# A sixth key tile for VectorE in the last 256 queries of a two-layer transformer kernel, with another opening and another order

## The chip, the cores and the metric

The kernel runs on one core of a Trainium2 chip, in one launch. The metric is device time in microseconds (us); lower is better. The engines are TensorE (PE; its weight loads are PEld), VectorE (DVE), ScalarE (ACT), GpSimd (POOL) and SyncE (SP, which issues the DMAs).

## The reference

```python
def reference(A_x, A_wqkv, A_wo, B_x, B_w1, B_b1, B_w2, B_b2):
    # _A_ref: attention, 32 heads of 16, over S=2048 rows of D=512, then @ wo
    #   scores = q k^T / 4;  p = softmax(scores);  o = p v
    # _B_ref: gelu(x @ w1 + b1) @ w2 + b2, hidden width F=1792
    x = A_x
    x = x + _A_ref(_layernorm(x, axis=-1), A_wqkv, A_wo)
    x = x + _B_ref(_layernorm(x, axis=-1), B_w1, B_b1, B_w2, B_b2)
    x = x + _A_ref(_layernorm(x, axis=-1), A_wqkv, A_wo)
    x = x + _B_ref(_layernorm(x, axis=-1), B_w1, B_b1, B_w2, B_b2)
    return x
```

Both layers use the same weights. Inputs and output are bfloat16.

## The kernel before

**Cells.** Attention is cut into cells: 128 keys (one of 16 key tiles `kt`) by 512 columns of scores. A pass is one segment of queries, one group of heads `g`, all 16 key tiles and four row groups `a`, so 64 cells. A segment is 512 queries; the last 512 queries of layer one are two segments of 256, in which a cell holds two heads side by side. There are 2048 cells in each layer. A cell's score is one matmul of 512 columns into a PSUM bank (L1432). Then its exponential is taken in one of two ways:

- ScalarE: one ACTIVATE over two or three banks at once (L1879) writes the unnormalized weights into units of a ring `pt`, or into units lent from other tensors that are dead at the time (`kt`, `q`, `g`, `v` in the profile's names). Then follows one matmul with V (PV).
- VectorE: one tensor_scalar (L1601) turns the scores into the bits of a rough exponential in a buffer `du` (or one lent from `kt`, `v`); GpSimd makes three shifted variants of it with two 64-bit integer adds for each pair of cells (L1691, L1695). Four PV matmuls follow, one with V and three with copies of V scaled by the weights `VW`, which `vcopies` makes (L1363). Only the tiles in `KD[l]` (five in each layer) have such copies and may go this way; a cell of theirs that nobody has taken when a pass runs out goes to ScalarE too.

PV matmuls (L1945) accumulate in one bank; PE puts matmuls with a zero matrix beside them where row groups are missing (L1953), and fillers where it would idle (L1420). In the last two segments PV and the first feed-forward product run in widths of 256 columns.

**Around attention.** When a segment's attention is done, `norm` divides and transposes on VectorE (L1000 to L1018), `wo` projects and adds (L1046), `ln` normalizes (L779 to L828), `hpair` makes the first feed-forward product (14 chunks, 16 matmuls each, L647 through `quads`; VectorE adds b1, L1155, or for the last segment ScalarE does all, L1150), `gelu` runs over half of the chunks at a time (L1176, with a table load before and after), and `ytile` makes the second product and adds (L1207). These run among the next segment's attention; for the last two segments part or all of it is left to the end. The opening loads tiles of x, normalizes the first four with GpSimd's power (L791), transposes them on PE (L844), projects K and Q, and starts.

**What sets the order.** A planner in the kernel, run when the program is built, goes through generators with assumed durations and priorities and writes out one fixed list of instructions and waits for each engine (`_Sched.run`). `KNOBS` are its parameters; `PICKS` chooses a row of `ORDERS` for each `STRETCH` of 24 us of its own clock. `SW` is the assumed cost of a change of PE's tiling mode. [...] On the chip there is no scheduler: each engine runs its list in order and waits for semaphores.

Of the kernel before, what the change touches and what calls it, by code (L numbers as in the profile page):

```python
# [5 lines left out]
ALU = mybir.AluOpType  # L6
ACT = mybir.ActivationFunctionType
BF16 = mybir.dt.bfloat16
# [6 lines left out]
D = 512  # L15
H = 32
# [14 lines left out]
W_MORE = 4  # L31
XT = 8
# [20 lines left out]
NKD = 5  # L53
QAT = (0, 200, 240, 280)
# [56 lines left out]
)  # L111
STRETCH = 24
PICKS = (1, 13, 1, 1, 13, 13, 1, 2, 1, 13, 1, 13, 13, 1, 1, 14, 1, 13, 13, 13, 13, 11, 3, 1,
         1, 13, 13, 13, 13, 13, 13, 1, 13, 13, 13, 1, 13, 1, 1, 1, 1, 3, 13, 13, 5, 1, 13, 13,
         1, 0, 1, 1, 13, 13, 13, 13, 1, 1, 1, 13)
# [141 lines left out]
HOLDP = 0.35  # L257
HOLDT = 0.2
# [5 lines left out]
class _Sched:  # L264
# [5 lines left out]
    def __init__(self, P):  # L270
        self.P = P
        self.clock = {e: 0.0 for e in P.ENGS}
        self.end = {}
# [68 lines left out]
    def _ready(self, op):  # L342
        t = 0.0
        for k in op.reads:
            if k not in self.P.lastw:
                return None
        for ev in self.P.deps(op.reads, op.writes):
            if op.eng == "pe" and ev[0] == "pe":
                continue
            t = max(t, self.end.get(ev, 0.0) - OWN * (op.eng == "dve" == ev[0]))  # L350
        if op.eng == "pe" and op.mode != self.mode:
            t -= SW
        if op.eng == "pool":
            if HOLDP and self.held_off(max(t, self.clock["pool"])):
                op.limit = 0.0
                return None
            if op.limit == 0.0:
                op.limit = self.port_ops[-1][1] + LATENCY["dve"]
            if op.limit < 1e9:
                t = max(t, op.limit)  # L360
            t = max(t, self.last(max(t, self.clock["pool"]))[0])
        if op.port and op.eng == "dve":
            at = max(t, self.clock["dve"])
            for a, b in self.pool_ops[-6:]:
                if a < at + HEAD and at < b - HEAD:
                    at = t = b - HEAD
        return t

# [67 lines left out]
    def run(self):  # L436
        while True:
# [75 lines left out]
SW = 0.107  # L513
# [5 lines left out]
def bass_interleave_layers__mha_block__dense_activation_gelu__prompt_kernel(  # L519
# [15 lines left out]
    with ExitStack() as es:  # L535
# [40 lines left out]
        T["VC"] = sb([128, NKD, 3, H * 17], BF16, "vc")  # L576
# [60 lines left out]
class _Plan:  # L637
# [12 lines left out]
    def init(self):  # L650
# [5 lines left out]
        yield _Op("pool", 0.1, lambda e: e.memset(T["IDENT"][:], 0.0), writes=["IDENT"])  # L656
# [3 lines left out]
        yield _Op("pool", 0.2, lambda e: e.memset(T["DU"][0][:, 0, 0, :].bitcast(BF16), 1.0), writes=["DU.0.0.0"])  # L660
# [6 lines left out]
        yield _Op("dve", 0.1, lambda e: e.tensor_reduce(  # L667
# [388 lines left out]
    def wloads(self):  # L1056
# [16 lines left out]
        for i, (l, seg) in enumerate(order):  # L1073
            todo = [((l, seg, "1", p), cols(hbm["w1"], 256 * p), 2) for p in range(NFC // 2)]
            tail = l == NL - 1 and seg[0] == self.NQ - 1
            if not tail:
                todo += [((l, seg, "2", (t, p)), rows(hbm["w2"], 256 * p, 0, D), 1) for t in self.tiles(seg) for p in range(NFC // 2)]
# [83 lines left out]
    def gelu(self, l, seg):  # L1161
# [8 lines left out]
        for f in range(0, NFC, half):  # L1170
# [4 lines left out]
            yield _Op("act", 0.065 + 0.4267 * half * n / 512 + ((1 if f == 0 else 0) + (0 if f == 0 or tail else 1)) * 1.31,  # L1175
                      lambda e, g=g: e.activation(out=g, in_=g, func=ACT.Gelu_apprx_tanh), reads=gk, writes=gk, prio=2)  # L1176
            for p in range(f // 2, (f + half) // 2):
                yield ("give", ("g", l, seg, p))

    def ytile(self, l, seg, t):  # L1180
# [5 lines left out]
        b = None if tail else (yield ("need", ("w", l, seg, "2", (t, 0))))  # L1186
# [3 lines left out]
        for p in range(NFC // 2):  # L1190
# [4 lines left out]
            else:  # L1195
                piece = (NL - 1, self.segs[NL - 1][-1], "2", last) if tail else (l, seg, "2", (t, p))
# [3 lines left out]
            for j in range(2):  # L1200
                fns += self.quads(pb, T["G"][:, 2 * p + j, q], ws[j], not (p or j), p == last and j == 1)
            yield _Op("pe", len(fns) // 4 * MM, fns, reads=[wk] + ["G.%d.%d" % (f, t % 4) for f in (2 * p, 2 * p + 1)],
                      writes=["B.%d" % b], prio=MID if p else FPRIO, mode="P")
# [119 lines left out]
    def setup_attention(self):  # L1323
# [4 lines left out]
        for pi, (l, seg, g, kts, part, final) in enumerate(self.pas):  # L1328
            self.alist.append([(pi, kt, a) for kt in kts if kt not in KD[l] for a in range(4)])
            self.dlist.append([(pi, kt, a) for kt in kts if kt in KD[l] for a in range(4)])  # L1330
# [5 lines left out]
        self.vuse = {(l, kt): sum(c[1] == kt for p, q in zip(self.pas, self.dlist) if p[0] == l for c in q) for l in range(NL) for kt in KD[l]}  # L1336
# [16 lines left out]

    def vcopies(self):
        T = self.T
        for l in range(NL):
            for j, kt in enumerate(KD[l]):
# [4 lines left out]
                for i, w in enumerate(VW):  # L1362
                    yield _Op("dve", 0.31, lambda e, j=j, i=i, w=w, src=src: e.tensor_scalar(  # L1363
                        T["VC"][:, j, i, :], src, w, 1.0, op0=ALU.mult, op1=ALU.mult),
                        reads=["V%d.%d" % (l, kt), self.vone(l, kt)], writes=["VC.%d.%d" % (j, i)])
                yield ("give", ("vc", l, kt))
            self.lend = 1

# [37 lines left out]
    def filler(self, b, mode):  # L1406
        T = self.T
        src = self.source()
        if src == ["VC.0.0"]:
            lhs, rhs = T["VC"][:, 0, 0, 0:128], T["VC"][:, 0, 0, 0:512]  # L1410
        else:
            lhs, rhs = T["IDENT"], T["DU"][0][:, 0, 0, :].bitcast(BF16)
# [289 lines left out]
    def copied(self, cell, du, jj, i):  # L1702
# [7 lines left out]
        else:  # L1710
            j = KD[l].index(kt)
            ws, wk = [T["VC"][:, j, i - 1, 17 * h:17 * h + 17] for h in hs], ["VC.%d.%d" % (j, i - 1)]
# [81 lines left out]
    def lend_units(self):  # L1794
# [9 lines left out]
        for u in range(*self.blocks[self.gblock - 1]):  # L1804
            yield ("rel", "pt", u)
# [91 lines left out]
    def pvs(self):  # L1897
        T = self.T
        pools = self.s.pools
        for pi, (l, seg, g, kts, part, final) in enumerate(self.pas):  # L1900
# [21 lines left out]
            def build(op, start, pi=pi, b=b, l=l, cols=cols, begun=begun, n=n):  # L1922
                op.fns, op.reads, rounds = [], [], 0
                while rounds < ROUNDS:
# [24 lines left out]
                    if rest and (warm or end):  # L1949
                        rhs = T["VC"][:, 0, 0, 0:512] if warm else T["ONES1"][:, 0:1].to_broadcast([128, 512])  # L1950
# [107 lines left out]
```

## Time and profile before

| What | Value |
|---|---|
| Time, median of 3 runs | 1429.25 us (1429.19 to 1429.66) |
| The profiled execution's own time | 1429.75 us |
| Its span, first to last instruction | 1427.9 us |
| Busy: PE, DVE, ACT, POOL | 1385.5, 1216.6, 1401.1, 997.9 us |
| Granted TensorE clock | 1.00 |
| DMA | 103.47 MB, 72 GB/s on average |

Columns of a row that groups instructions: line, engine, operation, tiles out<-in, shapes, count, then busy time and mean ns of one, then the engine's idle time before them and who ended it. A timeline row has start, duration, engine, line, operation, tiles, count, and in brackets the idle time before it. A row of stages has the stretch, its length, then busy time and instructions of PE, PEld, DVE, ACT and POOL, the clock, the share of DMA and GB/s. A row of waits has who waited, for whom, the total, the number of times and the longest. Records of one engine can overlap, so a duration can be longer than the time that an instruction adds.

### The profile page before, as it was taken

How to read it: one execution, taken by the hardware profiler on the slowest of the kernel's cores; microseconds unless marked ns; L12 is line 12 of the kernel's file. 1: busy time of each engine (PE TensorE's matmuls, PEld its weight loads, DVE VectorE, ACT ScalarE, POOL GpSimd, SP SyncE). 2: the span in 40 equal slices, each digit the busy share in tenths (PEclk: the TensorE clock that was granted, in tenths of full speed). 3: DMA queues.
4: the chain of work that ended last, by engine and by line, in shares of the span. 5: the costliest groups of instructions: out<-in, count | busy, mean ns of one | idle time of the engine just before them, and what ended most of it. 6: DMA issues, size and time to landing. Idle time of an engine off the chain costs nothing.

```text
span 1427.9 us, 45603 instructions
## 1 busy us (share of the span) xinstructions
PE 1385.5 (97%) x19402; PEld 420.7 (29%) x19402; DVE 1216.6 (85%) x2293; ACT 1401.1 (98%) x1406; POOL 997.9 (70%) x1256
## 2 busy tenths in 40 slices
PE   8999999999999999999999999999999999999999
PEld 3222222222222222222222222222222222344346
DVE  7789999788997889987998678899869977898684
ACT  7999999999999999999999999999999999999995
POOL 1086988668786787876767667757767977788661
PEclk9999999999999999999999999999999999999999
DMA  6100001261121611115411161101162105421522
GB/s 176 45 2 2 2 16 39 62 183 54 46 39 53 187 60 39 39 31 157 119 39 46 53 187 59 31 14 33 39 189 79 32 24 168 145 32 40 175 75 89
DMA packets 145187, 103.47 MB, mean 72 GB/s; under 512 B 37084, under 2 KB 143964, under 8 KB 144988
## 3 DMA queue, kind: packets, MB, share of 16 engines
q1 hardware_dynamic: 144988, 100.57, 25.2%
q8 instruction: 156, 2.56, 0.8%
q14 instruction: 43, 0.35, 0.1%
HBM read 88.74 MB, written 4.19 MB: 65 GB/s over the span
## 4 chain that ended last, share of the span: by engine, by line
ACT 67%; PE 24%; DVE 7%; POOL 2%; issue 1%; ACTq 0%; POOLq 0%
ACT pt L1879 50%; PE ps L1945 8%; PE ps L1432 8%; PE ps L647 7%; ACT q L1879 4%; ACT g L1879 3%; ACT g L1176 3%; ACT v L1879 3%; DVE du L1601 3%; ACT kt L1879 2%; POOL du L1695 1%; DVE kt L1601 1%; PE ps L1420 1%; ACT L1879 1%; ACT L1176 1%
## 5 line engine op out<-in xcount | busy, mean ns | idle before, releaser
L1879 ACT ACTIVATE pt<-ps 128x1024 bf16<-128x1024 f32 (+1 forms) x1085 | 1091.2, 1168 | 1.3 <-PE ps L1432 0.4
L1601 DVE TENSOR_SCALAR du<-ps 128x512 uint16<-128x512 f32 x894 | 597.2, 684 | 112.5 <-PE ps L1432 107.9
L1432 PE MATMUL ps<-qp,kt 32*128 32x512 bf16 x4096 | 537.4, 384 | 18.5 <-ACT pt L1879 11.2
L1695 POOL INT64_ADD du<-du x454 | 464.6, 1025 | 72.9 <-DVE qp L1380 9.6
L1691 POOL INT64_ADD du<-du x454 | 273.6, 605 | 231.9 <-DVE du L1601 180.8
L1945 PE MATMUL ps<-du,vc 128*17 128x512 bf16 (+1 forms) x2979 | 360.3, 360 | 2.3 <-POOL du L1695 0.6
L1432 PEld LDWEIGHTS ps<-qp,kt 32*128 32x128 bf16 x4096 | 143.2, 91 | 569.6 <-ACT pt L1879 177.9
L1945 PE MATMUL ps<-pt,v 128*17 128x512 bf16 (+1 forms) x2621 | 306.5, 359 | 4.3 <-ACT pt L1879 2.7
L1945 PE MATMUL ps<-du,v 128*17 128x512 bf16 (+1 forms) x993 | 166.3, 360 | 3.6 <-DVE v L988 1.0
L647 PE MATMUL ps<-xf,wr 128*32 128x512 bf16 (+1 forms) x2272 | 162.0, 371 | 0.4 <-DMA xf<-pt 0.2
L1601 DVE TENSOR_SCALAR kt<-ps 128x512 uint16<-128x512 f32 x202 | 136.2, 683 | 22.0 <-PE ps L1432 20.6
L1945 PE MATMUL ps<-kt,vc 128*17 128x512 bf16 (+1 forms) x732 | 145.1, 344 | 0.8 <-POOL du L1691 0.8
L1945 PEld LDWEIGHTS ps<-du,vc 128*17 128x17 bf16 x2979 | 95.6, 89 | 81.4 <-issue 35.6
L1695 POOL INT64_ADD kt<-kt x104 | 105.3, 1013 | 15.7 <-DVE ra L797 3.8
L647 PE MATMUL ps<-wr,g 128*32 128x512 bf16 x1504 | 110.7, 383 | 1.1 <-ACT g L1176 1.1
L1945 PEld LDWEIGHTS ps<-pt,v 128*17 128x17 bf16 x2621 | 74.2, 88 | 79.1 <-issue 53.2
L1945 PE MATMUL ps<-v,vc 128*17 128x512 bf16 (+1 forms) x405 | 90.4, 351 | 0.1
L1155 DVE TENSOR_SCALAR g<-ps,hb1t 128x512 bf16<-128x512 f32 (+1 forms) x112 | 79.0, 706 | 10.2 <-PE ps L647 9.8
L1601 DVE TENSOR_SCALAR v<-ps 128x512 uint16<-128x512 f32 x116 | 78.2, 682 | 11.0 <-PE ps L1432 10.6
L1691 POOL INT64_ADD kt<-kt x104 | 62.3, 599 | 35.6 <-DVE kt L1601 17.2
L1879 ACT ACTIVATE q<-ps 128x1024 bf16<-128x1024 f32 (+1 forms) x78 | 82.0, 1128 | 0.0
L1945 PE MATMUL ps<-kt,v 128*17 128x512 bf16 (+1 forms) x334 | 79.4, 354 | 1.9 <-POOL du L1695 0.9
(108 smaller groups left out, 1462.4 us busy)
## 6 DMA issues: line engine op xcount, KB each, us to landing
wr<-in_B_w_dram SPq DMA_DIRECT2D x243, 256.0 KB, 3.1
wr<-in_A_wqkv_dram SPq DMA_DIRECT2D x24, 256.0 KB, 2.8
wr<-in_A_wo_dram SPq DMA_DIRECT2D x17, 256.0 KB, 3.0
x<-in_A_x_dram SPq DMA_DIRECT2D x7, 512.0 KB, 4.9
pt<-in_B_w_dram SPq DMA_DIRECT2D x13, 256.0 KB, 3.9
kept<-x SPq DMA_DIRECT2D x4, 512.0 KB, 3.1
x<-kept SPq DMA_DIRECT2D x4, 512.0 KB, 3.9
out_dram<-x SPq DMA_DIRECT2D x16, 128.0 KB, 2.9
```

Source lines behind the costliest of these rows:

```text
L647: return [lambda e, a=a: e.matmul(out[32 * a:32 * a + 32, :], lhsT=lhsT[:, 32 * a:32 * a + 32], rhs=rhs, start=start, stop=stop, tile_posi ...
L1155: yield _Op("dve", 0.21 + n / 966, lambda e, fc=fc, pb=pb: e.tensor_scalar(T["G"][:, fc, q], pb, T["HB1T"][:, fc:fc + 1], None, op0=ALU.ad ...
L1176: lambda e, g=g: e.activation(out=g, in_=g, func=ACT.Gelu_apprx_tanh), reads=gk, writes=gk, prio=2)
L1420: fns.append(lambda e, o=o, w=w, a=a, m=m: e.matmul(o, lhsT=w, rhs=rhs, start=start, stop=start, tile_position=(0, m * a)))
L1432: return (lambda e: e.matmul(o, lhsT=lhsT, rhs=rhs, start=True, stop=True, tile_position=(32 * a, 0)), ["K%d.%d.%d" % (l, gb, kt // 4), "Q ...
L1601: yield _Op("dve", 0.682, lambda e: e.tensor_scalar(u, self.bank(b), E_SCALE, E_BIAS, op0=ALU.mult, op1=ALU.add), reads=["B.%d" % b], writ ...
L1691: yield _Op("pool", 0.151 + 0.2176 * n, lambda e: e.int64_add(words(1, 1), words(0, 1), SHIFT * ONES), reads=key[0], writes=key[1])
L1695: yield _Op("pool", 0.143 + 0.4352 * n, lambda e: e.int64_add(words(2, 2), words(0, 2), 2 * SHIFT * ONES), reads=key[0] + key[1], writes=k ...
L1879: yield _Op("act", 0.052 + 0.4267 * n, lambda e, src=src, dst=dst: e.activation(out=dst, in_=src, func=ACT.Exp, scale=0.25), reads=["B.%d" ...
L1945: op.fns.append(lambda e, o=o, lhsT=q[0][0][m], rhs=q[0][1][:, n * m:n * m + n], a=a, st=st, sp=sp: e.matmul(o, lhsT=lhsT, rhs=rhs, start= ...
```

## The change

1. VectorE may also take key tile 13 (`EXTRA`) in the last segment of layer one (`ELATE` = 1). Its three scaled V copies are written by `vcopies` into layer zero's V, over four units that were lent to `pt` until then and are not lent any more.
2. The opening: the memset of the fillers' operand goes from GpSimd to VectorE; GpSimd's first powers (`early`) are not held for VectorE's port work; the engines' clocks begin at assumed values (`BEGIN`), and some assumed durations differ.
3. Other assumed durations: a table load 1.5 instead of 1.31, `SW` 0.109 instead of 0.107. `ORDERS` loses seven rows, and `PICKS` is another list: so the order of the whole program is another.
4. `ytile` and `wloads` go through `w2order`: for every second tile of a segment the pieces of w2 are loaded and used in reverse order. `W_SHARE` = 0, so no piece is shared between tiles.

```diff
+W_SHARE = 0
+EXTRA, ELATE = 13, 1
...
-PICKS = (1, 13, 1, 1, 13, 13, 1, 2, 1, 13, 1, 13, 13, 1, 1, 14, 1, 13, 13, 13, 13, 11, 3, 1,
+PICKS = (2, 2, 2, 2, 2, 0, 0, 0, 0, 0, 6, 6, 6, 6, 6, 1, 1, 1, 1, 1, 1, 1, 1, 1,
...
+BEGIN = {"pool": 0.72, "dve": 0.9, "act": 2.0, "sp": 0.12}
...
-        if op.eng == "pool":
+        if op.eng == "pool" and not self.early(op):
             if HOLDP and self.held_off(max(t, self.clock["pool"])):
...
+    def early(self, op):
+        return op.writes[0].startswith("RSTD") and self.clock["dve"] < HOT
...
-            if e == "pool" and op.writes[0] != "LIB":
+            if e == "pool" and op.writes[0] != "LIB" and not self.early(op):
...
-SW = 0.107
+SW = 0.109
...
-        T["VC"] = sb([128, NKD, 3, H * 17], BF16, "vc")
+        vc = sb([128, NKD, 3, H * 17], BF16, "vc")
+        T["VC"] = [vc[:, j, :, :] for j in range(NKD)] + [vf[0][:, 2048:2048 + 3 * H * 17].rearrange("p (i c) -> p i c", i=3)]
...
-        yield _Op("pool", 0.2, lambda e: e.memset(T["DU"][0][:, 0, 0, :].bitcast(BF16), 1.0), writes=["DU.0.0.0"])
+        yield _Op("dve", 0.35, lambda e: e.memset(T["DU"][0][:, 0, 0, :].bitcast(BF16), 1.0), writes=["DU.0.0.0"])
...
-            yield _Op("act", 0.065 + 0.4267 * half * n / 512 + ((1 if f == 0 else 0) + (0 if f == 0 or tail else 1)) * 1.31,
+            yield _Op("act", 0.065 + 0.4267 * half * n / 512 + ((1 if f == 0 else 0) + (0 if f == 0 or tail else 1)) * 1.5,
...
+    def w2order(self, l, seg, t):
+        odd = (t - self.tiles(seg)[0]) % 2
+        ps = range(NFC // 2)[::-1 if odd else 1]
+        return [(p, (l, seg, "2", (t - (i < W_SHARE and t > self.tiles(seg)[0]), p))) for i, p in enumerate(ps)]
...
+    def dtiles(self, l, seg):
+        return KD[l] + ((EXTRA,) if l == NL - 1 and seg in self.segs[l][len(self.segs[l]) - ELATE:] else ())
...
+        for gb in range(4):
+            yield ("need", ("otn", NL - 1, self.segs[NL - 1][0], gb))
+        lo = self.blocks[self.gblock - 1][0]
+        over = [k for u in range(lo + 4, lo + 8) for k in self.pkeys(u)]
+        yield from self.vcopy(NL - 1, EXTRA, NKD, over)
...
-        for u in range(*self.blocks[self.gblock - 1]):
+        lo = self.blocks[self.gblock - 1][0]
+        for u in range(lo, lo + 4):
             yield ("rel", "pt", u)
```

More of the change, by code (lines that the diff above doesn't have):

```diff
@@ L1076, in wloads @@
             if not tail:
-                todo += [((l, seg, "2", (t, p)), rows(hbm["w2"], 256 * p, 0, D), 1) for t in self.tiles(seg) for p in range(NFC // 2)]
+                for t in self.tiles(seg):
+                    pieces = self.w2order(l, seg, t)
+                    again = W_SHARE if t + 1 in self.tiles(seg) else 0
+                    todo += [(k, rows(hbm["w2"], 256 * p, 0, D), 1 + (i >= len(pieces) - again)) for i, (p, k) in enumerate(pieces) if k[3][0] == t]
             elif i == len(order) - 1:
@@ L1185, in ytile @@
             yield ("need", ("g", l, seg, p))
-        b = None if tail else (yield ("need", ("w", l, seg, "2", (t, 0))))
+        order = [(p, None) for p in range(NFC // 2)] if tail else self.w2order(l, seg, t)
+        b = None if tail else (yield ("need", ("w",) + order[0][1]))
         b = yield ("acq", "misc")
@@ L1189, in ytile @@
         q = slice((t % 4) * 128, (t % 4) * 128 + 128)
-        for p in range(NFC // 2):
+        for i, (p, piece) in enumerate(order):
             yield ("need", ("g", l, seg, p))
@@ L1195, in ytile @@
             else:
-                piece = (NL - 1, self.segs[NL - 1][-1], "2", last) if tail else (l, seg, "2", (t, p))
+                piece = (NL - 1, self.segs[NL - 1][-1], "2", last) if tail else piece
                 w = yield ("need", ("w",) + piece)
@@ L1200, in ytile @@
             for j in range(2):
-                fns += self.quads(pb, T["G"][:, 2 * p + j, q], ws[j], not (p or j), p == last and j == 1)
+                fns += self.quads(pb, T["G"][:, 2 * p + j, q], ws[j], not (i or j), i == last and j == 1)
             yield _Op("pe", len(fns) // 4 * MM, fns, reads=[wk] + ["G.%d.%d" % (f, t % 4) for f in (2 * p, 2 * p + 1)],
-                      writes=["B.%d" % b], prio=MID if p else FPRIO, mode="P")
+                      writes=["B.%d" % b], prio=MID if i else FPRIO, mode="P")
             if not tail or p == last:
@@ L1335, in setup_attention @@
                 self.pvleft[(pi, a)] = len(kts)
[L1336 removed]
+        self.vuse = {(l, kt): sum(c[1] == kt for p, q in zip(self.pas, self.dlist) if p[0] == l for c in q) for l in range(NL) for kt in KD[l] + (EXTRA,)}
         self.total, self.scored, self.nd, self.pa, self.pv = n, 0, 0, 0, 0
@@ L1367, in vcopies, with vcopy @@
             self.lend = 1
+        for gb in range(4):
[3 more added lines that the diff above has]
+        yield from self.vcopy(NL - 1, EXTRA, NKD, over)
+    def vcopy(self, l, kt, j, over=[]):
+        T = self.T
+        yield ("need", ("V", l, kt, kt // 4))
+        src = T["V"][l][:, kt, :, :].rearrange("p h c -> p (h c)")
+        for i, w in enumerate(VW):
+            yield _Op("dve", 0.31, lambda e, i=i, w=w: e.tensor_scalar(
+                T["VC"][j][:, i, :], src, w, 1.0, op0=ALU.mult, op1=ALU.mult),
+                reads=["V%d.%d" % (l, kt), self.vone(l, kt)], writes=["VC.%d.%d" % (j, i)] + over)
+        yield ("give", ("vc", l, kt))
     def qpad(self):
```

23 lines of the change are left out of this document (12 added, 11 removed), and 8 rows, old and new, of the table ORDERS.

## The prediction

> **What bounds the kernel now.** I read the page first, then the waits of ScalarE, then the timelines of the two ends, then the program order of both kernels.
>
> ```profile
> span 1427.9 us, 45603 instructions
> PE 1385.5 (97%) x19402; PEld 420.7 (29%) x19402; DVE 1216.6 (85%) x2293; ACT 1401.1 (98%) x1406; POOL 997.9 (70%) x1256
> ACT 67%; PE 24%; DVE 7%; POOL 2%; issue 1%; ACTq 0%; POOLq 0%
> L1879 ACT ACTIVATE pt<-ps 128x1024 bf16<-128x1024 f32 (+1 forms) x1085 | 1091.2, 1168 | 1.3 <-PE ps L1432 0.4
> ```
>
> The chain that ended last is ScalarE for two thirds of the span, and its exponentials have almost no idle time before them: 1.3 us over the largest group. So one asks where ScalarE does wait.
>
> ```profile
> ACT kt L852 <- PE ps L844: 6.7, 2, 6.2
> ACT xf L852 <- PE ps L844: 3.4, 1, 3.4
> ACT g L1150 <- PE ps L647: 3.2, 3, 2.2
> ACT pt L1879 <- PE ps L1432: 0.4, 2, 0.2
> ```
>
> The long waits are on lines of the opening (L852 into kt) and of the last feed-forward (L852 into xf, L1150). Hence three terms: the opening up to the first exponential; ScalarE's own work from there to the last one, which has nowhere to hide; and the tail behind the last one.
>
> **Opening.** [...]
>
> ```profile
> 1.67 0.52 POOL L660 MEMSET du<- 128x512 bf16 x1
> 2.25 5.72 PE L1420 MATMUL ps<-du,ident 128*128 128x512 bf16 x13 [2.25 <-POOL nhalf L661]
> 11.77 0.75 DVE L906 TENSOR_SCALAR qp<-ps,mask 128x512 bf16<-128x512 f32 x1 [0.79 <-PE ps L647]
> 12.04 0.09 PEld L728 LDWEIGHTS ps<-ident,b1c 14*128 14x128 bf16 x1 [0.50 <-DMA b1c<-in_B_b_dram]
> 12.56 0.58 ACT L912 CAST q<-ps 128x512 bf16<-128x512 f32 x1 [0.65 <-DVE qp L906]
> 12.58 0.11 PEld L1432 LDWEIGHTS ps<-qp,kt 32*128 32x128 bf16 x5 [0.45 <-DVE qp L906]
> 13.04 3.72 ACT L1879 ACTIVATE pt<-ps 128x1536 bf16<-128x1536 f32 x3
> ```
>
> Fillers can start about 0.45 earlier (memset gone from GpSimd's queue) and one of 0.44 (5.72/13) is gone: up to 0.9 us earlier on the PE. The new order also puts all 16 transposes ahead of the projections, and normalizes tile 0 later. But in both orders the transpose of b1c (L728) stands in PE's queue ahead of the first score, and it waited for its DMA until 12.04; nothing ahead of that DMA on SP's queue changes. What is late next is this landing: scores can go at about 12.25 instead of 12.58. I take -0.35, with the ends 0 and -0.9.
>
> **ScalarE's work.** Counted in the program order: exponentials of two tiles 1155 -> 1158, of three 191 -> 190, of one 1 -> 0; cells on ScalarE 2884 -> 2886, on VectorE 1212 -> 1210. The sixth tile is taken, but only for 6 of its 16 cells. Over all but the last 256 queries VectorE loses 8 (by segment of queries: -2, 0, -2, -6 in layer zero; +2, 0, 0, 0 in layer one), because the order is another. In ScalarE's slots the last 256 queries go from 68 two-wide, 13 three-wide and 1 single to 74, 7 and 0.
>
> ```profile
> 376.20 6.42 ACT g L1879 x7
> 35.32 1.11 ACT L1879 ACTIVATE pt<-ps 128x1024 bf16<-128x1024 f32 x1
> 36.22 1.55 ACT L1879 ACTIVATE kt<-ps 128x1536 bf16<-128x1536 f32 x1
> 37.55 34.98 ACT L1879 ACTIVATE pt<-ps 128x1024 bf16<-128x1024 f32 x30
> L1879 ACT ACTIVATE pt<-ps 128x1024 bf16<-128x1024 f32 x905 | 866.1, 1093 | 1.3 <-PE ps L1432 0.4 <-PE ps L1945 0.2
> L1879 ACT ACTIVATE pt<-ps 128x512 bf16<-128x512 f32 x1 | 0.7, 730 | 0.0
> 202.06 4.23 ACT L1879 ACTIVATE kt<-ps 128x1024 bf16<-128x1024 f32 x4
> 206.19 1.94 ACT L1879 ACTIVATE q<-ps 128x1024 bf16<-128x1024 f32 x2
> ```
>
> Records overlap, so a slot is the distance of starts or a run divided by its count: two-wide 6.42/7 = 0.917, three-wide 37.55 - 36.22 = 1.33; the single one I put at 0.73 less the overlap of 1.09 - 0.92, some 0.5. Sum: 3 x 0.917 - 1.33 - 0.5 = +0.9 us. The last 256 queries save 6 x 1.33 + 0.5 - 6 x 0.917 = 3.0, the rest pays 3.9; ScalarE being full in both, only the sum counts. Exponentials into the lent kt rows are slower (206.19 - 202.06 over 4 = 1.03, or 0.11 above 0.917) and rise from 43 to 54; not all are: between 0 and 1.2, taken +0.6. How well the new order feeds ScalarE can't be read beforehand: between -1.3 (the idle time above, all gone) and +4 (one wait as long as the xf one), taken 0.
>
> **The tail, where I see the cost.** The last score is issued when the bank of the exponential before it comes free; from there the PE has a fixed list of work.
>
> ```profile
> 1388.59 0.47 DVE L1155 TENSOR_SCALAR g<-ps,hb1t 128x256 bf16<-128x256 f32 x1
> 1399.78 0.09 PEld L1432 LDWEIGHTS ps<-qp,kt 32*128 32x128 bf16 x1 [0.22 <-ACT pt L1879]
> 1397.09 1.04 POOL L1695 INT64_ADD kt<-kt  x1
> 1401.38 1.28 ACT L1176 ACT_TABLE_LOAD   x1
> 1401.85 2.14 PE L647 MATMUL ps<-xf,wr 128*32 128x256 bf16 x72
> 1403.81 1.04 PE L647 MATMUL ps<-wr,otn 128*32 128x512 bf16 x16
> 1392.00:1401.40 9.40, 9.08 (x247) 6.11 (x248) 3.32 (x7) 9.38 (x9) 6.17 (x10) 1.00 0.67 199
> 1401.40:1412.70 11.30, 11.21 (x241) 6.75 (x236) 9.27 (x27) 5.25 (x4) 1.15 (x2) 1.00 0.27 80
> 1412.70:1425.10 12.40, 12.38 (x342) 8.84 (x332) 1.38 (x2) 6.00 (x14) 0.00 (x0) 1.00 0.08 25
> 1424.47 0.60 PE L647 MATMUL ps<-pt,g 128*32 128x512 bf16 x8
> 1425.13 0.69 DVE L1207 TENSOR_TENSOR x<-x,ps 128x512 bf16<-128x512 bf16 x1 [2.33 <-PE ps L647]
> ```
>
> The windows show PE at 11.21 of 11.30 and 12.38 of 12.40: from the last score (1399.78) to the last matmul (1425.07) PE is the bound, 25.3 us. A matmul of 256 columns costs (1403.81 - 1401.85)/72 = 0.0272 there; one of 512 columns twice that, as the last window agrees: 224 short and 112 long ones in 12.4 us make 448 units of 0.0277. Behind the last score stand, in such units, before: 26 of PV, 14 of zero fills, 320 of the first feed-forward product (96 of the 224 of the last segment but one, and 224 of the last), 64 of the output projection, 448 of the second product: 872, or 23.7 us; 1.6 us are left for 8 transposes and idle time. After: 66, 6, 416 (192 of those 224), 64 and 448: 1000 units. That is 128 more, +3.5 us.
>
> Why they end up there: before, ScalarE works through its last 22 cells (seven three-wide and the single) alone while VectorE has only the feed-forward copies left (7 instructions in 9.4 us), and PE fits 128 of the 224 matmuls between the scores, the first copied at 1388.59, 12.8 us before the last exponential ends at 1401.38. After, the sixth tile shortens that stretch; the layer norm of the segment ahead ends only 6 VectorE cells before the end, and just 32 of the 224 stand ahead of the last score. The last segment's PE work isn't shortened by ScalarE's saving: it is pushed behind it.
>
> One correction: the last score now stands ahead of a two-wide exponential behind a three-wide one, so the last exponential ends 1.33 + 0.92 - 0.22 = 2.03 us after it, before 1401.38 - 1399.78 = 1.60. From last exponential to last matmul: before 25.29 - 1.60 = 23.7; after 25.29 + 3.5 + 0.1 (second products behind a later gelu) - 2.03 = 26.9. Tail +3.2, with ends +2.3 (0.8 of the idle time gone as well) and +4.5 (PE waits 1.3 for the last norm, whose chain has one more copy in it).
>
> The copies of V are hidden:
>
> ```profile
> L1363 DVE TENSOR_SCALAR vc<-v 128x544 bf16<-128x544 bf16 x30 | 9.5, 346 | 0.0
> L1695 POOL INT64_ADD du<-du x22 | 22.0, 999 | 5.0 <-DVE ra L797 1.6 <-DVE ott L1009 1.3 <-DVE x L812 0.7
> L1691 POOL INT64_ADD du<-du x21 | 12.4, 591 | 11.1 <-DVE du L1601 8.7 <-DVE varr L784 1.4 <-DVE ott L1009 0.6
> ```
>
> Three at 0.35 are 1.0 us on an engine that is 85% busy, long ahead of their use; uncovered they would cost 1.0. The reversed order of the w2 pieces changes no number of loads or matmuls; as each piece is still loaded before its use, 0. Four lent units in dead V fewer cost nothing as long as others are free: exponentials into v0 go from 60 to 23 and those into pt rise. GpSimd has 1.6 us a pair (0.59 + 1.00); three more pairs in the last segment are 4.8 us and it idled 5.0 and 11.1 before these groups.
>
> **Sum.** -0.35 + 0.9 + 0.6 + 0 + 3.2 = +4.35 on the profiled execution's own 1429.75 (its span of 1427.9 and 1.85 around it), 1434.1; the median shown is 0.5 lower, so 1433.6.
>
> **Rivals.**
> Room on the PE (not slower): the moved matmuls fall into gaps, the tail costs nothing, and what is left is -0.35 + 0.9 + 0.6 = +1.15: 1430.4. It decides if PE's rows in the tail are longer than its work. For it: weight loads fill only 6.75 of 11.30 and 8.84 of 12.40 us. [...] Chance 0.2.
> Late feeding (slower still): GpSimd's last pairs, now needed behind the last score, or starved exponentials in the middle cost about 4 more: 1437.6. For it: GpSimd's last add ends at 1398.13, before the last score, and by the order it would not any more. Chance 0.16.
> The sixth tile does what it is named for: VectorE relieves ScalarE in full, 3.0 us off and nothing paid elsewhere, PE with room: 1429.25 - 0.35 - 3.0 = 1425.9. Against it are the counts (two cells more on ScalarE in all). Chance 0.05. My forecast has 0.59.
>
> **Numbers.** What a measurement can tell from no change is 0.2%, 2.9 us: 1426.4 to 1432.1. Low end: -0.9 + 0.9 + 0 - 1.3 + 2.3 = +1.0, 1430.2. High end: 0 + 0.9 + 1.2 + 2.5 + 4.5 = +9.1, 1438.3. That leaves out the last rival and little else. Faster 0.05; same is the room rival and the low flank of the forecast, 0.2 + 0.05 = 0.25; slower 0.70.
>
> **What would show it.** Right: the first exponential at 12.6 to 12.8; the last one ending near 1402.5; some 27 us of nearly gapless PE from there to the last matmul, with 72 short matmuls behind the last PV as before but 104 ahead of it. Wrong: a last exponential ahead of 1399 (order feeds better than I think) or after 1406 (worse); a tail below 24 us behind it (room on the PE); GpSimd's adds as PE's releaser behind the last score (late feeding).

## The result, and the profile after

| | Median, us | Range, us | Ratio to the kernel before |
|---|---|---|---|
| Before, beside it | 1429.66 | 1429.19 to 1430.70 (5 runs) | |
| Changed kernel | 1436.22 | 1434.78 to 1437.52 (5 runs) | 1.0046, interval 1.0035 to 1.0058 |

The changed kernel is 6.6 us slower; forecast were +4.35 and 1433.6. Its profiled execution is the longest of its five, 1437.52 (span 1435.7), so its trace holds about 1.3 us more than its median.

Lines of the page of the changed kernel: span, busy time, the chain that ended last by engine, the largest group of exponentials.

```profile
span 1435.7 us, 45584 instructions
PE 1394.7 (97%) x19423; PEld 424.7 (30%) x19423; DVE 1213.5 (85%) x2295; ACT 1402.3 (98%) x1407; POOL 999.2 (70%) x1247
ACT 54%; PE 35%; DVE 8%; POOL 1%; issue 1%; DMA 1%; SPq 0%; POOLq 0%; ACTq 0%
L1907 ACT ACTIVATE pt<-ps 128x1024 bf16<-128x1024 f32 (+1 forms) x1100 | 1104.2, 1167 | 3.2 <-PE ps L1459 2.3
```

ScalarE's share of the chain falls from 67% to 54% and PE's rises from 24% to 35%: more of the time is spent where PE is late. The exponentials of this group now wait 3.2 us instead of 1.3.

The opening of the changed kernel, from the timelines of PE and ScalarE, and the first piece of its chain:

```profile
1.77 5.30 PE L1447 MATMUL ps<-du,ident 128*128 128x512 bf16 x12 [1.77 <-POOL nhalf L661]
12.68 0.18 PE L728 MATMUL ps<-ident,b1c 14*128 14x14 bf16 x1 [1.78 <-DMA b1c<-in_B_b_dram]
13.14 3.90 ACT L1907 ACTIVATE pt<-ps 128x1536 bf16<-128x1536 f32 x3 [0.82 <-PE ps L1459]
15.48 1.90 PE L647 MATMUL ps<-kt,g 128*32 128x512 bf16 x16
```

```profile
4.71 7.93 DMA b1c<-in_B_b_dram
```

The fillers start 0.48 us earlier (1.77 instead of 2.25) and one is gone, as foreseen, but the first exponential starts at 13.14, not before 13.04. PE waits 1.78 us for the DMA of b1c, though `qp`, the operand of the scores behind it in its list, is done at 11.71, and goes on at 12.68; in the trace of before it went on at 12.05. Then PE works at half its pace, with a granted clock of 0.50 from 14.3 to 17.7 us: 16 matmuls take 1.90 us, where before they took 1.05.

The end, from the timelines of DVE, PE and ScalarE (first copy of the feed-forward product, last score, table load behind the last exponential, last run of feed-forward matmuls, last add), then the rows of stages from the last score to the last matmul, before and after:

```profile
1401.42 0.48 DVE L1158 TENSOR_SCALAR g<-ps,hb1t 128x256 bf16<-128x256 f32 x1 [0.91 <-PE ps L647]
1402.61 0.39 PE L1459 MATMUL ps<-qp,kt 32*128 32x512 bf16 x2
1404.82 1.28 ACT L1179 ACT_TABLE_LOAD   x1
1408.00 2.23 PE L647 MATMUL ps<-xf,wr 128*32 128x256 bf16 x72
1432.90 0.69 DVE L1216 TENSOR_TENSOR x<-x,ps 128x512 bf16<-128x512 bf16 x1 [2.34 <-PE ps L647]
```

```profile
1399.80:1425.10 25.30, 25.19 (x622) 16.85 (x618) 11.43 (x30) 12.83 (x20) 1.15 (x2) 1.00 0.21 63
```

```profile
1402.60:1432.90 30.30, 29.58 (x755) 21.71 (x751) 14.27 (x36) 13.43 (x20) 5.63 (x9) 1.00 0.35 103
```

The last exponential ends 3.44 us later (1404.82 against 1401.38), and from there to the end of the span it takes 30.9 us instead of 26.5: +4.4. Together that is the 7.8 us between the two spans. PE is busy 29.58 of 30.30 us behind the last score, with 755 matmuls instead of 622. The first feed-forward copy comes 12.8 us later than before (1401.42 against 1388.59).

The 3.44 us ahead of the last exponential can be split. A slot is the median distance of ends: 0.917, 1.343 and 0.490 us for exponentials of two, three and one tiles, 3.141 for a gelu, 1.301 for a table load, 0.479 for a cast. From the first exponential to the end of the last the slots sum to 1381.20 us before and 1382.12 after (+0.92). The rest, time that ScalarE lost, is 0.18 before and 1.50 after up to 48 us (+1.3), and 6.95 and 8.03 from 48 us on (+1.1). The start of the first exponential adds 0.1.

### The profile page after: what moved, and what is told of

It reads as the page before. It is cut to its first block, busy times and chain, and to the rows that moved or that the text cites. A ratio compares the mean times of both kernels' runs of the same rounds, so it can differ in the third digit from the quotient of the medians.

```text
span 1435.7 us, 45584 instructions
## 1 busy us (share of the span) xinstructions
PE 1394.7 (97%) x19423; PEld 424.7 (30%) x19423; DVE 1213.5 (85%) x2295; ACT 1402.3 (98%) x1407; POOL 999.2 (70%) x1247
## 4 chain that ended last, share of the span: by engine, by line
ACT 54%; PE 35%; DVE 8%; POOL 1%; issue 1%; DMA 1%; SPq 0%; POOLq 0%; ACTq 0%
ACT pt L1907 42%; PE ps L1973 12%; PE ps L1459 12%; PE ps L647 11%; ACT q L1907 3%; DVE du L1628 3%; ACT g L1179 3%; ACT g L1907 2%; ACT kt L1907 2%; ACT v L1907 1%; DVE kt L1628 1%; DMA b1c<-in_B_b_dram 1%; ACT L1907 1%; ACT L1179 1%; DVE ott L1009 0%
## 5 line engine op out<-in xcount | busy, mean ns | idle before, releaser
L1907 ACT ACTIVATE pt<-ps 128x1024 bf16<-128x1024 f32 (+1 forms) x1100 | 1104.2, 1167 | 3.2 <-PE ps L1459 2.3
L1459 PE MATMUL ps<-qp,kt 32*128 32x512 bf16 x4096 | 543.2, 384 | 16.8 <-ACT pt L1907 7.8
L1973 PE MATMUL ps<-du,vc 128*17 128x512 bf16 (+1 forms) x2946 | 344.8, 359 | 2.2 <-POOL du L1722 0.9
L1459 PEld LDWEIGHTS ps<-qp,kt 32*128 32x128 bf16 x4096 | 146.4, 91 | 577.5 <-issue 173.6
L1973 PE MATMUL ps<-pt,v 128*17 128x512 bf16 (+1 forms) x2658 | 289.5, 358 | 5.9 <-ACT pt L1907 4.0
L1973 PEld LDWEIGHTS ps<-du,vc 128*17 128x17 bf16 x2946 | 90.6, 89 | 84.0 <-issue 38.1
L1973 PEld LDWEIGHTS ps<-pt,v 128*17 128x17 bf16 x2658 | 69.7, 88 | 84.0 <-issue 55.3
L1907 ACT ACTIVATE q<-ps 128x1024 bf16<-128x1024 f32 (+1 forms) x86 | 90.2, 1130 | 0.0
L1973 PE MATMUL ps<-v,vc 128*17 128x512 bf16 (+1 forms) x417 | 87.2, 350 | 1.2 <-POOL du L1722 0.8
```

The costliest lines, as they stand in the source:

```text
L1459: return (lambda e: e.matmul(o, lhsT=lhsT, rhs=rhs, start=True, stop=True, tile_position=(32 * a, 0)), ["K%d.%d.%d" % (l, gb, kt // 4), "Q ...
L1907: yield _Op("act", 0.052 + 0.4267 * n, lambda e, src=src, dst=dst: e.activation(out=dst, in_=src, func=ACT.Exp, scale=0.25), reads=["B.%d" ...
L1973: op.fns.append(lambda e, o=o, lhsT=q[0][0][m], rhs=q[0][1][:, n * m:n * m + n], a=a, st=st, sp=sp: e.matmul(o, lhsT=lhsT, rhs=rhs, start= ...
```

## The experiments

All twelve; the columns from the fourth on are from profiled executions. A profiled execution can be off the median of its kernel: by +1.3 us in the changed kernel, by +4.1 in e12, by less than 0.8 in the others. "Lost" is the time that ScalarE lost between its slots, up to 48 us and after. "Tail" runs from the table load behind the last exponential to the end of the span. "Units" are matmuls of 256 columns behind the last score, by the program order. The kernel before was 1429.66 to 1429.90 beside them.

| Kernel | Median, us | Interval of the ratio | First exp. | Lost | Last exp. ends | Tail | Units |
|---|---|---|---|---|---|---|---|
| before | 1429.25 | | 13.04 | 0.18 + 6.95 | 1401.38 | 26.5 | 872 |
| changed | 1436.22 | 1.0035 to 1.0058 | 13.14 | 1.50 + 8.03 | 1404.82 | 30.9 | 1000 |
| e1 b1c early | 1435.75 | 1.0031 to 1.0056 | 12.04 | 0.64 + 7.99 | 1402.81 | 30.9 | 1000 |
| e2 before, b1c late | 1433.18 | 1.0013 to 1.0036 | 14.28 | 2.52 + 6.98 | 1405.00 | 26.6 | 872 |
| e3 no sixth tile | 1435.16 | 1.0027 to 1.0052 | 12.70 | 0.56 + 8.50 | 1406.45 | 27.3 | 880 |
| e4 no sixth, b1c early | 1435.04 | 1.0023 to 1.0049 | 12.21 | 0.89 + 8.36 | 1406.15 | 27.3 | 880 |
| e5 order alone | 1436.14 | 1.0027 to 1.0052 | 12.59 | 0.17 + 9.48 | 1407.06 | 27.3 | 872 |
| e6 order back | 1436.94 | 1.0040 to 1.0065 | 12.44 | 0.32 + 12.92 | 1403.57 | 31.4 | 1040 |
| e7 order back, no sixth | 1438.14 | 1.0037 to 1.0062 | 11.76 | 0.51 + 16.21 | 1409.75 | 27.4 | 864 |
| e9 order back, b1c early | 1437.29 | 1.0036 to 1.0064 | 11.80 | 0.98 + 13.38 | 1404.03 | 31.5 | 1040 |
| e10 before, four units | 1434.80 | 1.0022 to 1.0049 | 12.03 | 0.18 + 7.15 | 1401.14 | 31.3 | 1016 |
| e11 units back | 1429.75 | 0.9992 to 1.0010 | 11.99 | 0.24 + 7.11 | 1400.56 | 26.6 | 872 |
| e12 sixth, other picks | 1429.46 | 0.9987 to 1.0005 | 12.19 | 2.11 + 10.37 | 1402.54 | 29.2 | 960 |
| e13 units back, one pick | 1428.15 | 0.9977 to 0.9996 | 11.84 | 0.38 + 7.71 | 1399.94 | 26.6 | 872 |

### The opening: e1 and e2

Only SyncE's list is edited, behind the planner, so that every other list stays as it is.

```diff
 # e1, changed kernel: b1c between wq and wv
+        sp = P.prog["sp"]
+        sp.insert(6, sp.pop(8))
 # e2, kernel before: b1c behind the third load of x
+        sp = P.prog["sp"]
+        sp.insert(11, sp.pop(8))
```

> Changed kernel, with the DMA of b1c issued between those of wq and wv instead of behind the second load of x; every list but SyncE's is the same. Theory (the opening lost its time to the late landing of b1c: PE idle for 1.8 us ahead of the first score, then at half pace for some 3 us): b1c lands by 10, PE does not wait for it, the first exponential starts at 11.9 to 12.4 instead of 13.14, the 16 projection matmuls that took 1.90 us take 1.05, ScalarE's starved time in the first 48 us falls from 9.5 to 6 or less, and the time falls by 2.5 to 3.5 us, to about 1433.2. Rival one (only the landing was late, the half pace has another cause): first exponential at about 12.3 but the slow matmuls stay, -0.8, 1435.4. Rival two (the opening's lateness is made good further on, as PE is gapless and the end hangs on PE): no change, 1436.2.

> Kernel before, with the DMA of b1c issued behind the third load of x; nothing else differs. Theory (an idle stretch of about 2 us on PE in the opening makes the PE go at half pace for a while afterwards): b1c lands near 13.3, PE idles from 11.7 to 13.3, the first exponential starts at about 13.8 instead of 13.04, the 16 projection matmuls behind it take about 1.9 us instead of 1.05, and the time rises by 2.5 to 3.5 us, to about 1432.5. Rival one (no half pace): +0.8, 1430.4. Rival two (made good later): no change, 1429.6.

The timelines of e1, PE and ScalarE, and then of e2:

```profile
10.83 0.16 PE L730 MATMUL ps<-ident,b1c 14*128 14x14 bf16 x1
11.58 0.60 PE L1461 MATMUL ps<-qp,kt 32*128 32x512 bf16 x5 [0.59 <-DVE qp L908]
12.04 3.72 ACT L1909 ACTIVATE pt<-ps 128x1536 bf16<-128x1536 f32 x3
13.87 1.16 PE L649 MATMUL ps<-kt,g 128*32 128x512 bf16 x16
```

```profile
13.59 0.19 PE L730 MATMUL ps<-ident,b1c 14*128 14x14 bf16 x1 [2.73 <-DMA b1c<-in_B_b_dram]
14.28 2.37 ACT L1881 ACTIVATE pt<-ps 128x1536 bf16<-128x1536 f32 x2 [1.97 <-PE ps L1434]
17.80 1.90 PE L649 MATMUL ps<-kt,g 128*32 128x512 bf16 x16
```

In e1 the wait is gone, the score waits for `qp` instead, the slow matmuls are gone, and the span is 2.0 us shorter than that of the changed kernel's profiled execution. But the median falls only by 0.5, where 2.5 to 3.5 were expected. The clocks of the single executions suggest why: of the five of the changed kernel only the two longest, 1437.23 and 1437.52 (the profiled one), show a mean granted clock of 0.999; the other three, the median among them, show 1.000 and took 1434.78 to 1436.22. So the half pace is not in the median. In e2 a wait of 2.73 us brings the half pace into the kernel before: the first exponential comes 1.24 later, ScalarE loses 2.3 more up to 48 us, and the median rises by 3.4. Here six of the seven executions show a clock of 0.998 or 0.999, and the seventh is the shortest, 1431.19. So the effect is shown, and its size for the changed kernel is 2 us at most, about 0.5 in the median.

### The sixth tile: e3 and e4

```diff
 # e3; e4 has e1's edit besides
-EXTRA, ELATE = 13, 1
+EXTRA, ELATE = 13, 0
```

> Changed kernel without the sixth tile for VectorE (ELATE = 0); the plan is the same up to the last 256 queries. ScalarE gets six cells back: two-wide exponentials 74 to 68, three-wide 7 to 13, which is 6 x 1.33 - 6 x 0.917 = +2.5 us; behind the last score PE has 880 units of 256 columns instead of 1000, which is 120 x 0.0272 = -3.3 us. Theory (the end hangs on PE, which works without gaps, so that the sixth tile only moves PE's work behind the last score): the last exponential ends some 2.5 us later, the tail behind it is about 3 us shorter, and the time is that of the changed kernel within 1 us, 1435.2 to 1436.7. Rival (ScalarE's relief counts in full, the tail does not grow by it): +2.5, 1438.7. Second rival (the sixth tile is what made it slower): back by 4 or more, 1432.

> Changed kernel without the sixth tile and with the DMA of b1c issued between those of wq and wv. If the opening and the sixth tile act apart, the sum of the two single runs: theory -3.0 for the opening, -0.5 for the sixth tile, 1432.7, which is still 3 us above the kernel before, left to the other order. If the end hangs on PE alone, the early start is lost again: 1435.7.

Timelines of e3 (PE, ScalarE) and its row of stages behind the last score:

```profile
12.24 0.18 PE L728 MATMUL ps<-ident,b1c 14*128 14x14 bf16 x1 [1.55 <-DMA b1c<-in_B_b_dram]
12.70 3.71 ACT L1907 ACTIVATE pt<-ps 128x1536 bf16<-128x1536 f32 x3 [0.59 <-PE ps L1459]
14.53 1.05 PE L647 MATMUL ps<-kt,g 128*32 128x512 bf16 x16
1406.45 1.28 ACT L1179 ACT_TABLE_LOAD   x1
```

```profile
1403.90:1430.90 27.00, 25.88 (x634) 17.57 (x630) 12.20 (x31) 13.81 (x20) 1.15 (x2) 1.00 0.24 69
```

Without the sixth tile ScalarE has 2.55 us more to do and its last exponential ends later, while the tail is 3.6 us shorter: the tile trades one for the other. The medians, 1435.16 against 1436.22 and (b1c early) 1435.04 against 1435.75, say that it costs 1.1 and 0.7 us, which the intervals can't tell from nothing. The theory of e3 holds; neither the tile's relief nor the tile itself is the 6.6 us. In e4 the early b1c adds nothing in the median (-0.1, where 3.0 were expected).

### The order and the units: e5 and e10

e5 is the kernel before with the changed `PICKS` and `ORDERS`, `SW` and table load, and nothing else. e10 is the kernel before with four units fewer lent, and nothing else.

```diff
 # e5
-PICKS = (1, 13, 1, 1, 13, 13, 1, 2, 1, 13, 1, 13, 13, 1, 1, 14, 1, 13, 13, 13, 13, 11, 3, 1,
+PICKS = (2, 2, 2, 2, 2, 0, 0, 0, 0, 0, 6, 6, 6, 6, 6, 1, 1, 1, 1, 1, 1, 1, 1, 1,
...
-SW = 0.107
+SW = 0.109
...
-... ((1 if f == 0 else 0) + (0 if f == 0 or tail else 1)) * 1.31,
+... ((1 if f == 0 else 0) + (0 if f == 0 or tail else 1)) * 1.5,
 # e10
-        for u in range(*self.blocks[self.gblock - 1]):
+        lo = self.blocks[self.gblock - 1][0]
+        for u in range(lo, lo + 4):
```

> Kernel before with the changed kernel's PICKS and ORDERS, SW = 0.109 and the table load at 1.5, and nothing else of the change: the order alone. By the program order ScalarE gets 1158 two-wide, 192 three-wide and no single exponentials instead of 1155, 191 and 1, VectorE 8 cells fewer: 3 x 0.917 + 1.343 - 0.49 = +3.6 us of work; behind the last score stand 872 units of 256 columns, as before. Theory (the order is what costs): +3.6 for ScalarE's work, +1.2 for time lost between exponentials from 48 to 1392 us as in the changed kernel, tail and opening unchanged: 1434.5. Rival (the sixth tile and the opening cost, the order is neutral as its gain elsewhere pays for the cells): 1430.

> Kernel before with one edit: of the eight units in layer zero's dead V only four are lent to pt, as in the changed kernel; no sixth tile, no copies, same opening, same PICKS. Counted: two-wide 1162, three-wide 187, +0.6 us of ScalarE's work; 1016 units of 256 columns behind the last score against 872, +3.9 less some 0.4. Theory (the four missing units make the 5.7 us wait of an exponential near 1303 us that the kernels with the order put back show): a wait of ScalarE for a unit of 1 us or more between 1200 and 1392 us and a time of 1433.5 to 1437. Rival (the units are free, the wait comes of the copies or of the reversed w2 pieces): 1430.

e10, timelines of DVE and ScalarE (last layer norm of the segment ahead, table load) and its row of stages; after it the same layer norm in the kernel before:

```profile
1393.55 0.74 DVE L828 TENSOR_SCALAR pt<-x,rstd,nmr 128x512 bf16<-128x512 bf16 x2
1401.14 1.28 ACT L1176 ACT_TABLE_LOAD   x1
```

```profile
1398.80:1429.50 30.70, 29.72 (x766) 20.82 (x762) 14.64 (x37) 13.55 (x20) 2.22 (x5) 1.00 0.34 101
```

```profile
1382.24 0.40 DVE L828 TENSOR_SCALAR pt<-x,rstd,nmr 128x512 bf16<-128x512 bf16 x1
1383.20 0.37 DVE L828 TENSOR_SCALAR pt<-x,rstd,nmr 128x512 bf16<-128x512 bf16 x1
```

The order alone costs 6.3 us: 3.6 of ScalarE's work by the counts, the rest mostly between the slots (2.5, where 1.2 were expected) and in the tail (0.8). Four units fewer alone, in the old order, cost 5.1 us. My expectation was right on that time and wrong on where: no exponential waits over 0.4 us for a unit. The last score is 0.9 us earlier than before (1398.85; the opening of that execution was 1.0 earlier), but the layer norm of the segment ahead ends 10.7 us later (1394.29 against 1383.57), so that all 448 feed-forward matmuls of the last two segments stand behind the last score. The tail shows it: 31.3 us.

The two do not add. Both are in e3, which has the new opening and the reversed w2 order besides and is no slower than e5 (1435.16 and 1436.14). In the new order the missing units show no price, but that order has one of its own.

### The old order with the rest of the change: e6, e7 and e9

e6 is the changed kernel with `PICKS`, `ORDERS`, `SW` and the table load of before; e9 has b1c early besides; e7 is e9 without the sixth tile.

```diff
 # e6, e7 and e9: the lines of e5's diff taken back in the changed kernel
 # e7 and e9 besides
+        sp = P.prog["sp"]
+        sp.insert(6, sp.pop(8))
 # e7 besides
-EXTRA, ELATE = 13, 1
+EXTRA, ELATE = 13, 0
```

> Changed kernel with PICKS, ORDERS, SW and the table load's 1.31 of the kernel before; sixth tile, opening and reversed w2 order stay. Counted: two-wide 1168, three-wide 180, so ScalarE's work is 3.34 us less than before; the sixth tile is taken for 10 cells, VectorE has 8 cells more; behind the last score stand 1040 units of 256 columns instead of 872, +168 x 0.0272 = +4.6. Theory (the end hangs on PE): -3.3 + 4.6 - 0.4 (last score further ahead of the last exponential's end) + 0 to 1.5 for the opening's late b1c = about +1.5, 1431.3. Rival (the sixth tile relieves in full): 1429.8 - 3.3 = 1426.5.

> As the kernel with the order put back, but without the sixth tile, and b1c's DMA issued between those of wq and wv: what is left of the change is the opening and the reversed w2 order. Counted: two-wide 1160, three-wide 188, +0.06 us of work; 864 units behind the last score, -0.2. Theory: first exponential 1.0 earlier than before, half of that lost again in the first 48 us: -0.6, 1429.2, a little faster than before. Rival (an earlier start is lost on the way, or the reversed w2 order costs loads): 1430 or more.

> The kernel with the order put back and b1c's DMA issued between those of wq and wv; beside the one without the sixth tile it gives the price of the sixth tile alone in the order of before, with the same opening. Counted between the two: ScalarE's work -3.40, units behind the last score 1040 against 864, +4.8 us, less some 0.4. Theory (PE bound end): +1.0 against the one without, 1430.2. Rival (relief in full): -3.4 against it, 1425.8.

ScalarE's timeline in e6, and its longest wait in the stages before the tail:

```profile
1296.67 1.45 ACT L1915 ACTIVATE v<-ps 128x1536 bf16<-128x1536 f32 x1
1303.75 2.37 ACT L1915 ACTIVATE pt<-ps 128x1536 bf16<-128x1536 f32 x2 [5.63 <-PE ps L1981]
```

```profile
ACT pt L1915 <- PE ps L1981: 5.8, 2, 5.6
```

All three miss their expectation by 6 to 9 us. One wait is 5.63 us of it in each: at 1303.75 in e6 an exponential into the ring `pt` waits, by the profile for a PV, which frees its unit. PE does not idle meanwhile: it is busy 6.00 of the 6.00 us from 1298 to 1304 with what stands ahead of that PV in its list. The same wait is in e7, which has no sixth tile. So the tile is not its cause. What these kernels have in common against the kernel before is the four units fewer with the extra copies in their place (the expectation of e7 leaves these two out), the opening and the reversed w2 order.

In e7 there is more. From PE's timeline, and a stage behind it:

```profile
1238.58 0.27 PE L1983 MATMUL ps<-kt,vc 128*17 128x256 bf16 x1 [2.42 <-issue]
```

```profile
1240.20:1243.50 3.30, 3.30 (x37) 0.85 (x38) 2.71 (x6) 2.35 (x3) 1.65 (x2) 0.50 0.02 5
```

PE stands still for 2.42 us without anything in the profile that it waited for (0.52 at the same place in e9), then the granted clock is 0.50 for 3.4 us, and ScalarE waits 2.5 us and twice 0.5. This does not happen in every execution: three of e7's five show a mean clock of 0.999, and they are the longest, 1438.14 to 1438.87; the shortest took 1435.00. So e9 against e7 (-0.9 in the median, where +1.0 was expected for the sixth tile in the old order) is no measure of the tile.

### Units back, and the best order found: e11, e12 and e13

```diff
 # e11: e7 with eight units lent and without the extra copies
-        yield from self.vcopy(NL - 1, EXTRA, NKD, over)
...
-        for u in range(lo, lo + 4):
+        for u in range(*self.blocks[self.gblock - 1]):
 # e12: e9 with other rows in four entries of PICKS (23, 49, 51, 52)
-1 ... 0 ... 1, 13
+10 ... 3 ... 5, 15
 # e13: e11 with another row in entry 23 of PICKS
-1
+10
```

> As the kernel with the order put back, without the sixth tile and with b1c early, but all eight units in dead V are lent again and the three extra copies are gone: of the change only the opening and the reversed w2 order are left, with b1c's DMA between those of wq and wv. Counted: ScalarE's work and the 872 units behind the last score are those of before. Theory (units were the cause): no wait near 1303; the first exponential 1.0 to 1.2 earlier than before, 0.3 to 0.5 of it lost again in the first 48 us, tail as before: -0.7, 1429.1. Rival (the reversed w2 order or the opening has a price further on): 1431 or more.

> Sixth tile, four units lent, opening and reversed w2 order as in the changed kernel, SW, table load and PICKS of before except for four stretches (23, 49, 51 and 52 take rows 10, 3, 5 and 15), b1c's DMA between those of wq and wv. Counted: two-wide 1168, three-wide 180, -3.3 us of ScalarE's work; 960 units behind the last score against 872, +2.4 less 0.4; opening -0.7. Theory (the sixth tile pays only where the order avoids the wait for units, and gives back on PE most of what it takes from ScalarE): no wait over 1 us near 1300, -3.3 + 2.0 - 0.7 = -2.0, 1427.9. Rival (four units are too few in any order like that of before): 1433 or more. Second rival (relief in full): 1425.9.

> No sixth tile, eight units lent, PICKS of before but for stretch 23, which takes row 10; opening, reversed w2 order and b1c's DMA between those of wq and wv as before it. Counted: two-wide 1161, three-wide 186, one single: VectorE takes three cells more and ScalarE's work is 6 x 0.917 - 5 x 1.343 = -1.2 us; 872 units behind the last score, as before. Theory (with the tail unchanged, what VectorE takes from ScalarE counts in full): 1429.7 - 1.2 = 1428.5, and without the sixth tile it is at least as fast as the kernel with the sixth tile and the same row in stretch 23 (1429.46). Rival (PE, not ScalarE, sets the end, and three cells more on VectorE cost it as much as they save): 1429.7.

With the units back and the copies out the wait is gone and 8.4 us with it: e11 is 1429.75, where e7 was 1438.14. Part of that is e7's half pace: against e7's shortest execution it is 5.3 us, about the wait. The opening and the reversed order of w2 together are worth nothing that can be measured (0.9992 to 1.0010), though e11's first exponential starts at 11.99. The table suggests why: the opening of before started its first exponential at 13.04 in one execution and at 12.03 in another (before, e10; in e5, with the new order, at 12.59), so that 13.04 was a late one.

e12 shows that neither the sixth tile nor the four units fewer need cost anything: with four picks changed the kernel is level with before, 7.8 us ahead of e9 (1437.29), from which it differs by these picks alone. It misses its expectation of 1427.9, and of the kernels without the tile it is level with e11 (1429.75) and behind e13 (1428.15). Its profiled execution was the longest of the eleven, 1433.55, and the only one with a clock of 0.999: PE stood still for 1.85 us near 1236, and the clock was 0.50 from 1239.2 to 1242.7. So its row in the table shows more lost time than its median holds.

e13, without the sixth tile, is the only kernel ahead of before: 1428.15, ratio 0.9977 to 0.9996; the slowest of its eleven executions took 1428.48, the fastest of the fourteen of before beside it 1428.73. Its end:

```profile
1399.94 1.28 ACT L1187 ACT_TABLE_LOAD   x1
```

```profile
1398.30:1423.60 25.30, 25.21 (x623) 16.84 (x618) 11.49 (x30) 12.89 (x20) 1.16 (x2) 1.00 0.22 64
```

It gives VectorE three cells more in the middle, 1.2 us less for ScalarE, and leaves the 872 units behind the last score alone. By the medians it is 1.6 us faster than e11, so that what VectorE took counts in full. Between the two profiled executions it is 0.8, as ScalarE lost 0.7 more between its slots.

## Why the prediction was right, and where its steps were not

The direction was right, by the two terms that were read from the program order; the size was 2.2 us short (+4.35 forecast, +6.6 in the medians, +7.8 between the two traces, to which the terms below refer).

- **Opening: wrong.** Forecast -0.35, ends 0 and -0.9; in the trace +1.4 (0.1 in the start, 1.3 lost up to 48 us). The dependence was named rightly: with this opening the first exponential starts 0.46 us behind the landing of b1c in three executions (12.68 and 13.14; 12.24 and 12.70, the forecast's own 12.6 to 12.8; in e6 11.98 and 12.44). What failed is that the landing was taken as fixed at 12.04 and that a PE which waits was taken to go on at full pace. In the median the step is worth 0 to 0.5 us (e1, e11).
- **ScalarE's work: right.** +0.9 forecast, +0.92 by the slots. That the stages ahead pay 3.9 and the last 256 queries give back 3.0 shows in the distances: the 3840th of 4096 scores, the last ahead of those queries, starts 5.7 us later than before (1313.8 and 1308.1; 1.4 of it from the opening), the last one 2.8.
- **Exponentials into kt rows and feeding: +0.6 forecast, +1.1 lost from 48 us on.** The slow ones among the kt rows take 0.19 us more each, 3.2 us in all instead of 2.7; the rest of the 1.1 is waits of 0.2 to 0.6 us. That is inside the end of +4 that was given. (That end was called as long as the xf wait, which is 3.4, and the high end of the sum takes 2.5 for it.)
- **Tail: right in mechanism, too small.** Forecast +3.2, trace +4.4, inside the end of 4.5. The 1000 units were there. The mis-sized part is their price: PE's busy time is 25.19/872 = 0.0289 us a unit before and 29.58/1000 = 0.0296 after, with transposes and changes of shape in it, against the 0.0272 of a run of equal matmuls; 128 x 0.0272 = 3.5, the rows differ by 4.4. And PE idles 0.72 instead of 0.11 us. Over all kernels of the table the tail goes with the units: 26.5 to 27.4 us at 864 to 880, 29.2 at 960, 30.9 at 1000, 31.3 to 31.5 at 1016 to 1040, about 0.029 a unit.
- **Cause of the tail: half right.** The text laid it to the sixth tile, which shortens ScalarE's last stretch. e3 confirms that trade. But e10 makes 1016 units without any sixth tile: the fewer units alone put the layer norm that late. And the tile's tail is not what makes the changed kernel slower than before: e5, the order alone, loses 6.3 of the 6.6 us with a tail of 27.3. With the sixth tile the loss stands in the tail, without it (e3) in ScalarE's work, and the time is nearly the same. The forecast added what it counted in both places, so its sum did not hang on the cause; that it came out with half of the cause wrong is luck.
- **Hidden at 0: wrong for the units.** "Four lent units in dead V fewer cost nothing as long as others are free" was priced from the counts of one order. In the old order they cost 5.1 us; in the new one nothing that shows, but that order costs 6.3; with four other picks (e12) nothing that shows either. The forecast came out because counts and units of the final lists were summed, whatever had led to them. The reversed w2 pieces are bounded by e11: nothing measurable there. The copies stand in no run alone; e12 has them and is level with before.
- **Rivals.** "Room on the PE" is out: weight loads fill 21.71 of 30.30 us of the tail, while the matmuls fill 29.58, and added units lengthen it at full price. So the 8.6 us of it without weight loads were not room. "Late feeding" is out as GpSimd's work: its adds end at 1407.05, but PE waited only 0.2 us for them; the starved exponentials that this rival also named came to 1.1 us of its 4. The sixth tile's full relief is out by e3.

What stays open: why four units fewer lead to so late a layer norm in e10, which the runs show without the planner's choice that turns it; where the 2.5 us between the slots of e5 come from; what PE stands still for near 1236 in e7 and e12; and whether the wait of e6 and e7 comes of the units alone, since e11 takes out the copies as well.

## What to carry to other kernels

When an order is planned against many resources, a buffer given up has no price of its own that could be read from whether others are free: here four lent units fewer cost 5.1 us in the old order and nothing that shows once the order was chosen with them (e12). Price such a change with the order planned anew, more than once: four picks alone moved the time by 7.8 us, more than the key tile could give (2.5 us of ScalarE's time, given back on PE). Before moving work from one full engine to another, count what stands behind the last item of the first engine on the second; where that count grows, the relief is only moved to the tail, and where it stays (e13), it counted in full in the medians. Take more than one execution of the opening before pricing a tenth of a microsecond there.

## What was not expected of the hardware

**Half pace after a short wait.** In the fourteen traces, from its first matmul on, PE idles four times for more than 1.6 us at a stretch: 1.78 us (changed kernel), 2.73 (e2), 2.42 (e7) and 1.85 (e12). In or behind each of these the granted clock falls to 0.50, for 3.4, 6.8, 3.4 and 3.4 us, and behind the first two 16 matmuls of 512 columns took 1.90 us instead of 1.05. It need not set in at once: in the changed kernel it does so at 14.3, 1.6 us after the wait is over. After waits of 1.40 (e6) and 1.55 us (e3), and after all shorter ones, it stays at 1.00. Over 13 to 48 us that is a mean clock of 0.95 in the changed kernel, where before it was 1.00:

```profile
13.00:48.00 35.00, 34.43 (x462) 10.51 (x457) 30.34 (x100) 33.82 (x33) 0.18 (x1) 0.95 0.42 94
```

```profile
13.00:48.00 35.00, 34.44 (x477) 10.90 (x476) 31.16 (x103) 35.00 (x36) 0.18 (x1) 1.00 0.43 98
```

So in these traces waits of 1.78 us and more brought the half pace and waits up to 1.55 us did not; what else decides it was not shown. The executions of one opening differ as well: the same 13 fillers of the opening of before took 5.72, 5.00, 4.86 and 4.56 us in four of them (before, e5, e2, e10), and what made the difference was not shown.

**A DMA that lands late by itself.** With the same issues ahead of it, b1c's 3.5 KB released PE at 11.46 to 12.68 us in six executions (11.46 in e10, 11.98 in e6, 12.05 before, 12.13 in e5, 12.24 in e3, 12.68 in the changed kernel).
